# Output products of the last octet in every fourth segment: a buffer of their own in two pieces, and the left V products behind them

## The chip, the cores and the metric

One NeuronCore of a Trainium2 chip. The metric is the device time of one execution in microseconds; lower is better. Before the change three runs took 1659.49, 1665.99 and 1658.9 us (median 1659.49).

## The reference, cut to what matters

The output is a gated mix of a recurrent attention (A) and a gated feed-forward layer (B) over the same 2048 rows of width 640.

```python
def _A_ref(x, mem0, Wq, Wk, Wv, Wo, seg_len):       # 32 heads of 192, M = 8, seg_len = 32
    mem = mem0
    for s in range(n_seg):                           # 64 segments
        xs = x[:, s * seg_len:(s + 1) * seg_len, :]
        h = jnp.concatenate([mem, xs], axis=1)       # 40 rows
        q, k, v = (jnp.einsum('btd,dhe->bhte', h, W) for W in (Wq, Wk, Wv))
        scores = jnp.einsum('bhqe,bhke->bhqk', q, k) * scale
        scores = jnp.where(mask, scores, -1e9)
        p = _softmax(scores, axis=-1)
        o = jnp.einsum('bhqk,bhke->bhqe', p, v)
        o = jnp.einsum('bhte,hed->btd', o, Wo)
        mem = o[:, :M, :]                            # the next segment's memory
        outs.append(o[:, M:, :])
    return jnp.concatenate(outs, axis=1)

def _B_ref(x, w_gate, w_up, w_down):
    h = _gelu(x @ w_gate) * (x @ w_up)
    return h @ w_down

g = _sigmoid((x * gate_w).sum(-1, keepdims=True))
out = g * _A_ref(...) + (1 - g) * _B_ref(...)
```

The first eight rows that a segment puts out are the memory rows of the next one, so the 64 segments follow each other strictly.

## The kernel before

The feed-forward part runs first, with its result in a scratch tensor in memory. Then come the 64 segments. All instructions are added to one list in the order of the program; a small scheduler derives the semaphore waits from the regions that each operation reads and writes, and each engine runs its own instructions in the order in which they were added. Nothing is reordered later, so the lists `PROG`, `PROG1` and `PROG3` in the source are the order.

A segment handles its 32 heads as four *octets* of eight. For each octet there are three projections (Q, K and V, each in five steps over the width with four 128x384 products side by side in the array: items `("g", n, k)`, lines 1134 and 226), the transposes of the Q and K rows on VectorE (`tq`, `tk`, line 1172), the scores (`sc`, lines 1183 to 1198), the softmax (`ex`), the transpose of its weights (`pt`, lines 1245 and 1250, copied by ACT at line 1257 and DVE at line 1259 for the last octet), the head outputs (`pv`, function `pv_oct`, lines 1278 and 1280) and their products with Wo (`wo`). The V rows are copied out of PSUM by ACT at line 1158. Item `("wo", i, 0)` handles the first half of octet i, `("wo", i, 1)` the second. Odd segments go through the octets backwards in the weights, so that half of the weights can stay where they are; the rest of them, 13 pieces of Q, K and V and three of Wo, are loaded during the segment into the slots of pieces that the segment has used (line 631, on the queue of SP).

Each segment has 32 rows of its own in this scheme: the 24 first rows of x and the eight memory rows. The eight last rows of x of four segments (the *left* rows) are put together: their Q, K and V rows are worked out for four segments at once (`lf`, `le`, `vb`; the left V products of the next four segments are line 967), and their head outputs wait in `uTl` until the last of the four. Hence a segment has a *place*, s % 4, and the fourth place (q == 3, program `PROG3`) differs: there the output products take 64 columns of head outputs (40 of this segment and 24 collected left ones) in function `wo_both`, line 1372, into one bank, LB. Their stationary operand is the buffer `U3` of 1536 bytes per partition. Three writers fill it in `pv_oct`: POOL with the left columns (line 1292, "U3l"), ACT with two of three chunks of the head outputs (line 1310, "uT evac") and DVE with the third in the last octet (line 1315, "uT mid"). There is one `U3` for all four octets, so those writers wait until the products of the octet before have read it. At places one to three the last octet's copies are made by halves instead (lines 1300 and 1304), each of two output products' operand.

The end of a segment of the fourth place runs through: `("wo", 2, 0)`, `("wo", 2, 1)`, `("pv", 3)`, three fifths of the left V products, `("wo", 3, 0)`, `("wo", 3, 1)`, the other two fifths. Behind it the sums in bank LB are copied by DVE (line 1561) and ACT (line 1564), DVE transposes them into the next segment's memory rows (line 1572) and with that the next segment's first projection may start. DVE mixes the outputs (lines 1083, 1431) with what POOL has scaled (lines 1081, 1089). ACT copies the left V rows (line 958).

The working memory behind all this is one tensor, cut by the tables `wsA_off` and `wsB_off`. In it `Q` holds the transposed Q rows of the octet at work (960 bytes), `p` its softmax weights (512 bytes) and, next to it, `Qz` a zero-padded copy of part of Q.

## Time and profile before

| | |
|---|---|
| median of three runs | 1659.49 us |
| the profiled execution's own time | 1669.24 us |
| its span, from the first to the last instruction | 1667.5 us |
| mean granted TensorE clock in it | 0.996 |
| TensorE busy | 1566.5 us, 94% of the span |
| VectorE, ScalarE, GpSimd busy | 60%, 47%, 33% |
| moved by DMA | 499.28 MB |

In the rows of the profile, PE is TensorE's products, PEld its weight loader, DVE is VectorE, ACT ScalarE, POOL GpSimd, and SPq the queue of SP, which only issues loads and stores. A row in order of time has the start and the length in us, the engine, the line of the source, the operation with its operands, how many of them are merged in it, and in brackets how long the engine was idle ahead of it and what ended that. A row of a wait has who waited for whom, the total, how many times, and the longest. In a chain of waits, each step leads to what released the step after it.

### The profile page before, as it was taken

To read this page: it belongs to the slowest core of one execution; us is meant where nothing else is said; L and a number is where in the kernel's file an instruction comes from. 1 tells how busy PE (TensorE), PEld (TensorE's weight loads), DVE (VectorE), ACT (ScalarE), POOL (GpSimd) and SP (SyncE) were. 2 spreads that over 40 slices of the span, in tenths; PEclk is the share of its full clock that TensorE was granted. 3 is DMA by queue.
4 is the path that set the end of the run, shared out by engine and by line. 5 is a ranking of instruction groups with operands and counts; after the bars stand their busy time and mean duration, and the time that the engine had idled before them with its cause. 6 is when DMAs were issued, how large, how long until landed. Compare 5 with 4: busy or idle time off the path is not lost.

```text
span 1667.5 us, 75813 instructions
## 1 busy us (share of the span) xinstructions
PE 1566.5 (94%) x37107; PEld 779.2 (47%) x28147; DVE 1000.1 (60%) x3023; ACT 785.5 (47%) x1874; POOL 549.9 (33%) x1609
## 2 busy tenths in 40 slices
PE   9999899999999999999999999999999999999986
PEld 4444345444444445444455444454444454444533
DVE  6453566656566666666565666566665656656653
ACT  2222454545555454545455554455454555545442
POOL 1110233333333333333333333333333333333332
PEclk9999999999999999999999999999999999999999
DMA  9915899888889898988889898889888898888984
GB/s 297 340 43 160 323 321 330 301 282 310 324 317 325 300 319 290 334 306 311 303 305 343 315 327 289 303 315 340 308 302 310 308 336 311 307 297 308 324 312 179
DMA packets 275415, 499.28 MB, mean 299 GB/s; under 512 B 121119, under 2 KB 136327, under 8 KB 275079
## 3 DMA queue, kind: packets, MB, share of 16 engines
q1 hardware_dynamic: 271000, 491.30, 84.2%
q8 instruction: 255, 4.18, 1.0%
q10 hardware_dynamic: 4079, 3.14, 0.6%
q14 instruction: 81, 0.66, 0.1%
HBM read 473.25 MB, written 21.09 MB: 296 GB/s over the span
## 4 chain that ended last, share of the span: by engine, by line
PE 71%; DMA 17%; DVE 6%; ACT 3%; issue 3%; SPq 1%; POOL 0%; DVEq 0%; ACTq 0%; POOLq 0%
PE ps L1134 19%; PE ps L226 17%; DMA arena<-in_A_Wv_dram 9%; PE ps L1372 7%; DMA arena<-in_A_Wo_dram 6%; PE ps L1328 5%; PE ps L1278 3%; PE ps L835 3%; PE ps L832 3%; PE ps L1354 2%; PE ps L1183 2%; PE ps L926 2%; PE ps L858 2%; PE ps L1191 1%; DMA arena<-in_A_Wk_dram 1%
## 5 line engine op out<-in xcount | busy, mean ns | idle before, releaser
L1134 PE MATMUL ps<-arena 128*32 128x384 bf16 x8640 | 645.6, 328 | 28.0 <-DVE arena L1572 11.6
L226 PE MATMUL ps<-arena 128*32 128x384 bf16 x8960 | 639.7, 326 | 2.7 <-ACT arena L1155 1.2
L1134 PEld LDWEIGHTS ps<-arena 128*32 128x32 bf16 x8640 | 231.9, 96 | 399.2 <-issue 258.9
L1172 DVE STREAM_TRANSPOSE arena<-arena 128x384 bf16<-128x384 bf16 x512 | 273.6, 559 | 70.5 <-ACT arena L1155 69.3
L1155 ACT ACTIVATE arena<-ps 128x384 bf16<-128x384 f32 x512 | 230.4, 493 | 99.0 <-PE ps L1134 93.8
L1328 PE MATMUL ps<-arena 128*32 128x320 bf16 x3456 | 184.4, 300 | 16.2 <-issue 11.1
L1175 POOL COPY arena<-arena 64x160 bf16<-64x160 bf16 x256 | 81.9, 320 | 334.3 <-DVE arena L1172 332.8
L1210 DVE TENSOR_REDUCE arena<-ps 104x4 f32<-104x160 f32 x256 | 82.9, 324 | 162.3 <-PE ps L1198 162.0
L1158 ACT ACTIVATE arena<-ps 128x384 bf16<-128x384 f32 x256 | 124.9, 488 | 88.2 <-PE ps L1134 88.2
L1263 ACT ACTIVATE arena<-ps 128x448 bf16<-128x448 f32 x192 | 104.4, 544 | 125.3 <-PE ps L1250 125.3
L1222 ACT ACTIVATE ps<-ps 104x160 f32<-104x160 f32 x256 | 74.8, 292 | 177.0 <-DVE ps L1212 175.2
L1310 ACT ACTIVATE arena<-ps 128x480 bf16<-128x480 f32 (+1 forms) x208 | 116.7, 561 | 87.4 <-PE ps L1280 86.1
L1008 POOL COPY arena<-arena 128x96 bf16<-128x96 bf16 x256 | 70.2, 274 | 246.7 <-PE ps L1198 174.4
L1224 DVE TENSOR_REDUCE arena<-ps 104x4 f32<-104x160 f32 x256 | 82.9, 324 | 83.8 <-ACT ps L1222 82.4
L1372 PE MATMUL ps<-arena 128*64 128x320 bf16 x1536 | 122.6, 307 | 0.5 <-ACT arena L1310 0.5
L1278 PE MATMUL ps<-arena 128*64 128x160 bf16 x1536 | 116.9, 240 | 5.6 <-ACT arena L1155 3.4
L1328 PEld LDWEIGHTS ps<-arena 128*32 128x32 bf16 x3456 | 89.6, 96 | 62.2 <-issue 19.1
L926 PE MATMUL ps<-arena 128*32 128x384 bf16 x1280 | 109.6, 328 | 1.1 <-issue 0.8
L1280 PE MATMUL ps<-arena 128*64 128x64 bf16 x1536 | 103.7, 193 | 2.3 <-issue 1.9
L1400 ACT ACTIVATE arena<-ps 128x384 bf16<-128x384 f32 x120 | 57.3, 490 | 101.2 <-PE ps L926 48.9
L1318 POOL COPY arena<-arena 128x96 bf16<-128x96 bf16 x192 | 51.7, 270 | 159.8 <-ACT arena L1300 88.7
L1278 PEld LDWEIGHTS ps<-arena 128*64 128x64 bf16 x1536 | 81.2, 109 | 37.6 <-ACT arena L1158 14.4
(102 smaller groups left out, 2362.6 us busy)
## 6 DMA issues: line engine op xcount, KB each, us to landing
arena<-in_A_Wk_dram SPq DMA_DIRECT2D x335, 384.0 KB, 6.5
arena<-in_A_Wv_dram SPq DMA_DIRECT2D x335, 384.0 KB, 8.7
arena<-in_A_Wo_dram SPq DMA_DIRECT2D x205, 480.0 KB, 6.0
arena<-in_A_Wq_dram SPq DMA_DIRECT2D x209, 384.0 KB, 5.5
arena<-left_qk_scratch SPq DMA_DIRECT2D x126, 96.0 KB
left_qk_scratch<-arena SPq DMA_DIRECT2D x49, 192.0 KB, 5.4
left_qk_scratch<-arena SPq DMA_DIRECT2D x30, 96.0 KB, 5.5
ffn_b_scratch<-arena ACTq DMA_DIRECT2D x16, 160.0 KB, 4.1
```

Source lines behind the costliest of these rows:

```text
L226: return e.add_instruction(mybir.InstMatmult(name=nm, start_tensor_calc=like["start"], stop_tensor_calc=stop, tile_size=(128, 32), tile_po ...
L926: fns.append(lambda e, outp=outp, rhs=rhs, j=j: e.matmul(outp, lhs, rhs, start=(k == 0), stop=(k == KT - 1), tile_position=(0, 32 * j)))
L1134: fns.append(lambda e, outp=outp, rhs=rhs, j=j: e.matmul(outp, lhs, rhs, start=(k == 0), stop=(k == KT - 1), tile_position=(0, 32 * j)))
L1155: S_.add("act", lambda e, m=m, bk=bk: e.activation(out=rows_sb[m], in_=ps[:, bk, 0:384], func=ACTF.Copy), reads=[r_ps[bk]], writes=[r_rows ...
L1158: S_.add("act", lambda e, i=i, bk=bk: e.activation(out=v_sb[i % NVB].rearrange("p (c n) -> p c n", c=3), in_=ps[:, bk, 0:384].rearrange("p ...
L1172: S_.add("dve", lambda e: e.transpose(out=dst[:, :, 0:L], in_=rows_sb[m].rearrange("p (c r) -> p c r", r=L)), reads=[r_rows[m]], writes=[r ...
L1263: S_.add("act", lambda e: e.activation(out=PT, in_=ps[:, bank, 0:PTW + 128], func=ACTF.Copy), reads=[r_ps[bank]], writes=[r_PT], name="pT ...
L1278: return [lambda e: e.matmul(full, v[:, e0:e0 + 64], PTm[:, i], start=True, stop=False, tile_position=(0, 64 * i), skip_group_check=True), ...
L1280: lambda e: e.matmul(part, vl[:, e0:e0 + 64], PTl[:, i], start=False, stop=True, tile_position=(0, 64 * i), skip_group_check=True)]
L1310: S_.add("act", lambda e: e.activation(out=apx(u[:, 0, 0, :], [[rs, na], [3 * rs, 4], [1, R]]), in_=ps[:, A, 0:na * W].rearrange("p (c t r ...
L1328: fns.append(lambda e, i=i, t=t, j=j, gv=gv: e.matmul(ps[32 * j:32 * j + 32, bank, 0:2 * DJ].rearrange("p (h n) -> p h n", h=2), lhs2[i], ...
L1372: S_.add("pe", [lambda e, i=i, g_=g_, c=c, p=p: e.matmul(ps[64 * i:64 * i + 64, LB, 0:2 * DJ], U3[:, p % 4, c, :], g_[:, c, 2 * DJ * i:2 * ...
```

## The change

The fourth octet at the fourth place no longer uses `U3`. It gets a buffer of two pieces of 768 bytes, `U3h`, one for each pair of output products, in memory that is free by then: `Q` for one, `p` and the start of `Qz` for the other. POOL copies the left columns in two pieces, and ACT and DVE copy the head outputs by halves, as at the other three places. `wo_both` reads the fourth octet's operand from the pieces. Since the fourth octet's copies need not wait for the third octet's output products any more, `PROG3` moves `("pv", 3)` between the two halves of them, and all five fifths of the left V products behind the last output product. The assertion that the diff changes had asked at the fourth place that each octet's output products stand ahead of the next octet's head outputs; it now asks that for the first two octets only.

```diff
--- before.py
+++ after.py
@@ -427,6 +427,10 @@
     U3 = bview(wsB_off["uT"], 1536).rearrange("p (t c r) -> p t c r", c=3, r=64)
     r_U3 = sreg(wsB_off["uT"], 1536)
     r_U3p = [[sreg(wsB_off["uT"] + x + 4 * i, 4) for x in (0, UB)] for i in range(3)]
+    U3h = [bview(wsB_off[nm], 768).rearrange("p (t c r) -> p t c r", c=3, r=64) for nm in ("Q", "p")]
+    r_U3h = [sreg(wsB_off[nm], 768) for nm in ("Q", "p")]
+    r_U3hp = [[[sreg(wsB_off[nm] + x + 4 * i, 4) for x in xs_] for i in range(3)] for nm, xs_ in (("Q", (0, 8)), ("p", (0, 256, 512)))]
+    assert wsB["Q"] >= 768 and wsB_off["p"] + 768 <= wsB_off["K"]
     st_f = [[fview(wsA_off["stats"] + (2 * b + i) * 16, 16) for i in (0, 0, 1)] for b in range(2)]
     r_st = [sreg(wsA_off["stats"] + 32 * b, 32) for b in range(2)]
     uTl = bview(wsB_off["uTl"], NCH * XA * 2).rearrange("p (c t) -> p c t", t=XA)
@@ -541,8 +545,8 @@
             ("sc", 2), ("g", 4, 0), ("g", 4, 1), ("g", 4, 2), ("g", 4, 3), ("pt", 1), ("tq", 3), ("wo", 0, 0),
             ("ex", 2), ("g", 4, 4), ("wo", 0, 1), ("tk", 3), ("pv", 1), ("g", 5, 0), ("pt", 2), ("sc", 3),
             ("wo", 1, 0), ("ex", 3), ("wo", 1, 1), ("pv", 2), ("g", 5, 1), ("g", 5, 2), ("g", 5, 3), ("pt", 3),
-            ("g", 5, 4), ("wo", 2, 0), ("wo", 2, 1), ("pv", 3), ("vb", 0), ("vb", 1), ("vb", 2), ("wo", 3, 0),
-            ("wo", 3, 1), ("vb", 3), ("vb", 4)]
+            ("g", 5, 4), ("wo", 2, 0), ("pv", 3), ("wo", 2, 1), ("wo", 3, 0), ("wo", 3, 1), ("vb", 0), ("vb", 1),
+            ("vb", 2), ("vb", 3), ("vb", 4)]
     PROG1 = [item for item in PROG if item != ("ex", 3)]
     PROG1.insert(PROG1.index(("pv", 2)), ("ex", 3))
     PROGS = (PROG, PROG1, PROG, PROG3)
@@ -1287,24 +1291,30 @@
         S_.add("pe", fns, reads=[r_v[o % NVB], r_vl[oc], r_PT], writes=[r_ps[A]] + ([r_ps[B]] if B != A else []), name="PVa s%d o%d" % (s, o))
         na = 2 if o in USPLIT else 3
         q = s % 4
-        if q == 3:
+        if q == 3 and o < NOCT - 1:
             u, ru = U3, r_U3p
             S_.add("pool", lambda e: e.tensor_copy(
                 out=U3.rearrange("p t c r -> p (t c) r")[:, :, R:64], in_=uTl[:, 12 * oc:12 * oc + 12, :]),
                 reads=[r_uTl[oc]], writes=r_U3p[2], name="U3l s%d o%d" % (s, o))
+        if q == 3 and o == NOCT - 1:
+            for h in ((0, 1), (1, 0))[s % 2]:
+                S_.add("pool", lambda e, h=h: e.tensor_copy(
+                    out=U3h[h].rearrange("p t c r -> p (t c) r")[:, :, R:64], in_=uTl[:, 12 * oc + 6 * h:12 * oc + 6 * h + 6, :]),
+                    reads=[r_uTl[oc]], writes=r_U3hp[h][2], name="U3l s%d o%d" % (s, o))
         if o == NOCT - 2 and s + 1 < NSEG:
             ek_copy(s, (3,))
-        if o == NOCT - 1 and q < 3:
+        if o == NOCT - 1:
             assert na == 2 and o % NUB == 1 and WOP == 4
+            uh, rh, rs = ([u[:, 2 * h:2 * h + 2] for h in range(2)], [[[x] for x in y] for y in r_uThp], R) if q < 3 else (U3h, r_U3hp, 64)
             for h in ((0, 1), (1, 0))[s % 2]:
                 S_.add("act", lambda e, h=h: e.activation(
-                    out=apx(u[:, 2 * h, 0, :], [[R, 2], [3 * R, 2], [1, R]]),
+                    out=apx(uh[h][:, 0, 0, :], [[rs, 2], [3 * rs, 2], [1, R]]),
                     in_=ps[:, A, 0:2 * W].rearrange("p (c t r) -> p c t r", t=4, r=R)[:, :, 2 * h:2 * h + 2], func=ACTF.Copy),
-                    reads=[r_ps[A]], writes=[r_uThp[h][0]], name="uT evac s%d o%d" % (s, o))
+                    reads=[r_ps[A]], writes=rh[h][0], name="uT evac s%d o%d" % (s, o))
                 S_.add("dve", lambda e, h=h: e.tensor_copy(
-                    out=u[:, 2 * h:2 * h + 2, 2, 0:R],
+                    out=uh[h][:, :, 2, 0:R],
                     in_=ps[:, B, 2 * W:3 * W].rearrange("p (t r) -> p t r", r=R)[:, 2 * h:2 * h + 2]),
-                    reads=[r_ps[B]], writes=[r_uThp[h][1]], name="uT mid s%d o%d" % (s, o))
+                    reads=[r_ps[B]], writes=rh[h][1], name="uT mid s%d o%d" % (s, o))
         else:
             rs = R if q < 3 else 64
             S_.add("act", lambda e: e.activation(
@@ -1368,12 +1378,13 @@
     def wo_both(s, item):
         for p in wo_pairs(s, item):
             g_, rg_ = piece(s, (3, p))
+            u, ru = (U3h[p % 4 // 2][:, p % 2], r_U3h[p % 4 // 2]) if item[1] == NOCT - 1 else (U3[:, p % 4], r_U3)
             for c in range(3):
-                S_.add("pe", [lambda e, i=i, g_=g_, c=c, p=p: e.matmul(
-                    ps[64 * i:64 * i + 64, LB, 0:2 * DJ], U3[:, p % 4, c, :], g_[:, c, 2 * DJ * i:2 * DJ * (i + 1)],
+                S_.add("pe", [lambda e, i=i, g_=g_, c=c, p=p, u=u: e.matmul(
+                    ps[64 * i:64 * i + 64, LB, 0:2 * DJ], u[:, c, :], g_[:, c, 2 * DJ * i:2 * DJ * (i + 1)],
                     start=(p == NWP - 1 and c == 0), stop=(p == 0 and c == 2), tile_position=(0, 64 * i),
                     skip_group_check=True) for i in range(2)],
-                    reads=[rg_, r_U3], writes=[r_ps[LB]], name="Wb s%d p%d" % (s, p))
+                    reads=[rg_, ru], writes=[r_ps[LB]], name="Wb s%d p%d" % (s, p))
 
     late_at = ("g", 1, KT - 1)
     r_lsth = [sreg(lst_off[3] + 768 * m, 768) for m in range(2)]
@@ -1383,7 +1394,7 @@
         g_end = {mi: at(("g", n, KT - 1)) for n, ms in enumerate(GROUPS) for mi in ms}
         assert g_end[(2, 1)] < at(("wo", 0, 0))
         assert at(("sc", 2)) < at(("pv", 1))
-        assert all(at(("wo", i, 1)) < at(("pv", i + (1 if x == 3 else 2))) for i in range(NOCT - (1 if x == 3 else 2)))
+        assert all(at(("wo", i, 1)) < at(("pv", i + (1 if x == 3 else 2))) for i in range(NOCT - 2))
         n_wos.append(at([item for item in prog if item[0] not in ("lf", "le", "vb")][-1]))
         for u in range(2):
             if ("le", x, u, 1) not in prog:
```

## The prediction

> **What bounds the kernel now.** I read the page's shares first, then the chain of work that ended last, then the stretches of the segments of the fourth place, and then each engine's order of time over the end of one such segment (985.60 to 1008.76), which I follow to the end of this text.
>
> ```profile
> PE 1566.5 (94%) x37107; PEld 779.2 (47%) x28147; DVE 1000.1 (60%) x3023; ACT 785.5 (47%) x1874; POOL 549.9 (33%) x1609
> DMA  9915899888889898988889898889888898888984
> ...
> PE 71%; DMA 17%; DVE 6%; ACT 3%; issue 3%; SPq 1%; POOL 0%; DVEq 0%; ACTq 0%; POOLq 0%
> ```
>
> TensorE carries 71% of the chain, and the loads 17%, at eight or nine tenths in nearly every slice. So a saving on TensorE counts only where no load ends the same stretch. The columns of the next rows are the stretch and its length, then the busy time and instructions of each engine, the granted clock and the share of the DMA.
>
> ```profile
> 340.53:367.24 26.71, 24.07 (x510) 12.60 (x390) 13.28 (x43) 11.89 (x29) 9.98 (x27) 0.94 0.79 270
> ...
> 985.60:1008.76 23.16, 22.31 (x509) 12.07 (x389) 13.22 (x43) 11.92 (x29) 9.51 (x26) 1.00 0.85 309
> ...
> sum 352.58, PE 337.08 PEld 182.30 DVE 197.76 ACT 178.44 POOL 143.48; mean PE 22.47 PEld 12.15 DVE 13.18 ACT 11.90 POOL 9.57
> ```
>
> Fifteen segments of the fourth place have a successor. Their sum is 352.58, or 23.5 each; most stand at 23.16, one at 26.71. A length that repeats so exactly is set by the program's own chain and not by loads, whose landing varies. The chain over the end of 985.60:1008.76 (start, length, what):
>
> ```profile
> 1003.02 1.75 PE ps L1372 x24
> ...
> 1005.07 0.87 PE ps L967 x12
> 1005.94 1.77 PE ps L1372 x24
> ...
> 1007.74 0.31 DVE arena L1561
> 1008.08 0.31 DVE arena L1561
> ...
> 1008.46 0.26 DVE arena L1572
> ```
>
> There is no DMA in it. It runs from the output products of the third octet through the head outputs, 12 left V products (L967) and the output products of the fourth octet (the second L1372) to the copies and the transpose that make the next segment's memory rows. What stands ahead of that second L1372 row is paid; what stands behind it, up to the transpose, is cover.
>
> **The change, part by part.** TensorE's starts and lengths, and the weight loader's, with the idle time ahead and its releaser:
>
> ```profile
> 1002.95 1.82 PE L1372 MATMUL ps<-arena 128*64 128x320 bf16 x24
> 1004.61 0.24 PE L1278 MATMUL ps<-arena 128*64 128x160 bf16 x2
> ...
> 1005.00 0.94 PE L967 MATMUL ps<-arena 128*32 128x384 bf16 x12
> 1005.87 1.82 PE L1372 MATMUL ps<-arena 128*64 128x320 bf16 x24
> 1007.62 0.51 PE L967 MATMUL ps<-arena 128*32 128x384 bf16 x8
> 1008.76 0.35 PE L1134 MATMUL ps<-arena 128*32 128x384 bf16 x4 [0.62 <-DVE arena L1572]
> ```
> ```profile
> 1005.60 0.10 PEld L967 LDWEIGHTS ps<-arena 128*32 128x32 bf16 x2 [0.33 <-ACT arena L1310]
> 1005.87 1.50 PEld L1372 LDWEIGHTS ps<-arena 128*64 128x64 bf16 x24 [0.17 <-issue]
> ```
>
> From the first output product of the third octet to that of the fourth pass 1005.87 - 1002.95 = 2.92 us: 1.66 for 24 products, 0.39 for the head outputs, 0.87 for the 12 left V products, which hold a stall of 0.33 for the ACT copy of the head outputs and 0.17 after it.
>
> *Left V products to the end.* The 0.87 goes out of this piece. The 12 products come back behind the last output product. There TensorE has 1008.76 - 1007.62 = 1.14 until the transpose lets the next segment begin, and 8 products in it. Eight of them took 0.51, and 12 products of the same shape 0.67 (next row), so each four add 0.16 and 20 take 0.99. They fit: cost 0, and 0.1 where they just do not.
>
> ```profile
> 1002.09 0.67 PE L1134 MATMUL ps<-arena 128*32 128x384 bf16 x12
> ```
>
> *Head outputs ahead of the second half of the third octet's output products.* The own buffer makes this legal; the 24 products are now 12, the head outputs, 12. One more change between kinds of product is needed; I bound it by 0 and 0.17 (the loader's idle time ahead of the second L1372, put down to issue) and take 0.02, since both kinds here load weights of the one shape 128x64. The head outputs move up by 12 products, 0.83, to 1003.8. Their inputs come from here:
>
> ```profile
> 1002.20 0.57 ACT L1310 ACTIVATE arena<-ps 128x480 bf16<-128x480 f32 x1 [1.04 <-PE ps L1280]
> 1002.88 0.44 ACT L1257 ACTIVATE arena<-ps 128x320 bf16<-128x320 f32 x1
> 1003.21 0.48 ACT L1158 ACTIVATE arena<-ps 128x384 bf16<-128x384 f32 x1
> ```
> ```profile
> PEld ps L1278 <- ACT arena L1158: 14.4, 30, 0.5
> ```
>
> The weights' copy ends at 1003.32, the V copy at 1003.69, 0.1 ahead of the new start. This edge was covered by the 12 products that now stand behind it, and the wait on it is real elsewhere (30 times, 14.4 us). The copy L1310 ended at 1002.77 and the output products that waited for it began at 1002.95, so a signal costs up to 0.18: bounds 0 and 0.19 a segment. I take 0.05, near the lower, since the copy ends first.
>
> *The copies in two pieces.* ACT and DVE copy two pieces of half the width:
>
> ```profile
> L1300 ACT ACTIVATE arena<-ps x96: 297/302/306, 197.7 to 1628.4; 128x160 bf16<-128x160 f32 x96
> ...
> L1304 DVE CAST arena<-ps x96: 228/236/244, 197.6 to 1628.3; 128x80 bf16<-128x80 f32 x96
> ```
>
> These are the same copies in the other three places (nanoseconds least, median, most). On ACT 2 x 0.30 stands for one copy of 0.44 (its place in time is between the end of the head outputs, 1005.0, and 1005.60, where the loader's wait for it ends); but the first piece is ready 0.30 after the head outputs, and the next 12 output products (0.83) cover it; the second has another 0.87, the 12 products that read the first piece, ahead of it. Were the 12 covering products gone, the stall of 0.33 would be back.
>
> *The left rows on POOL.* One copy that had to wait for the output products of the third octet becomes two that wait for POOL alone:
>
> ```profile
> 1003.16 0.29 POOL L807 COPY arena<-arena 128x120 bf16<-128x120 bf16 x1 [0.16 <-POOL arena L1448]
> 1004.84 0.43 POOL L1292 COPY arena<-arena 128x288 bf16<-128x288 bf16 x1 [1.39 <-PE ps L1372]
> ...
> 1006.93 0.69 POOL L1081 TENSOR_SCALAR arena<-arena 128x160 bf16<-128x160 bf16 x1 [0.17 <-POOL arena L1076]
> ```
>
> They run from 1003.45, at most 0.43 each, and are done by 1004.3. Three things wait for them: the last product of the third octet (the whole fourth octet is queued behind it), ACT's second piece, which writes beside one of them and could begin at 1004.6, and the products that read that piece; all come later, cost 0. The mixes behind them on POOL move up. The next segment's first POOL copy waits for TensorE, ACT and DVE besides, but for work that ends before the transpose it waits for anyway; behind it are the left rows and zeros for the first scores. SP's order is not changed.
>
> *Each boundary* then gains 0.87 less 0.02 for the extra change of product and 0.05 for V: 0.80. Fifteen give 12.0.
>
> *The last segment* has no left V products; its output products wait in the open.
>
> ```profile
> 1658.27 1.82 PE L1372 MATMUL ps<-arena 128*64 128x320 bf16 x24
> ...
> 1660.64 0.22 PE L1280 MATMUL ps<-arena 128*64 128x64 bf16 x1 [0.26 <-POOL arena L1292]
> ...
> 1661.38 1.82 PE L1372 MATMUL ps<-arena 128*64 128x320 bf16 x24 [0.53 <-ACT arena L1310]
> ```
>
> Both waits, 0.26 and 0.53, go behind the 12 products: 0.8 gained.
>
> *Late loads.* The fourth octet's last three output pieces are loaded in the same segment:
>
> ```profile
> 997.49 1.54 SPq L631 DMA_DIRECT2D arena<-in_A_Wo_dram  x3
> ...
> arena<-in_A_Wo_dram SPq DMA_DIRECT2D x3, 480.0 KB, 6.5
> ...
> arena<-in_A_Wo_dram SPq DMA_DIRECT2D x3, 480.0 KB, 7.3
> ```
>
> The last is issued by 999.03 and, at 6.5 or 7.3 us (the answers for this segment and for one 277 us later), lands at 1005.5 to 1006.3. It is needed by the last six output products, from 1007.2 before and 1006.4 after. It cannot land after 1007.2, or a wait would show before; so a boundary loses between 0 and 0.8. By the two answers it is 0 to 0.1 late: I take 0.07, 1.0 us for all.
>
> *Sum*: -12.0 - 0.8 + 1.0 = -11.8. The profiled execution took 1669.24 (span 1667.5 and 1.7 around it), so 1657.4 in its like; it is 9.8 over the median of the runs, 1659.49, and holds load stalls like 340.53:367.24 that the median need not have. From the median: 1647.7.
>
> **The rivals.** *The next place's loads take it back.* The first place's segments are not of one length:
>
> ```profile
> 367.24:389.56 22.32, 22.13 (x614) 11.21 (x474) 15.58 (x49) 10.64 (x27) 7.92 (x24) 1.00 0.88 314
> ...
> 1468.97:1492.78 23.81, 22.11 (x612) 11.33 (x473) 15.53 (x49) 10.75 (x28) 8.00 (x24) 1.00 0.84 294
> ```
>
> At equal TensorE work (22.1) they take 22.32 to 23.81, so loads do end some. If those loads went by the clock on the wall, 15 x 0.80 would be lost and 1658.7 remain; half of it, 1653. Against: a segment's loads are issued as its own products free their slots, so they begin earlier with it, and the DMA share of the fourth place (0.85) leaves room at its end. [...]
>
> ```profile
> DMA packets 290, 0.81 MB, mean 406 GB/s; under 512 B 32, under 2 KB 32, under 8 KB 288
> ```
>
> *The fourth octet's inputs end it.* If V costs its 0.19, the twenty left V products 0.1 and the last load 0.33 each time (between its 0 and 0.8), a boundary gains 0.87 - 0.62 = 0.25, and 1659.49 - 3.8 - 0.8 = 1654.9 results. For it: three margins of about 0.1; against: the exact 23.16.
>
> *Slower: a load stall that drops the clock.* In 340.53:367.24 the granted clock falls to 0.94, and the segment is 26.71 - 23.16 = 3.55 longer. If starting the products ahead of the last load turned its wait into such a drop, it would cost 3.55 in each segment struck: from four (14.2) it eats the gain, with six (21.3) the kernel is slower, with eight 1676. Against: the wait worked out above is tenths of a microsecond. [...]
>
> *It does not do what it says*: the output products of the fourth octet still start after the same wait. Then only the last segment's 0.8 is left, 1658.7.
>
> **How the numbers follow.** Forecast 0.60, own range 1645 to 1651. Loads take it back 0.16, inputs end it 0.10, clock drops 0.08, nothing done 0.06. Half a per cent, 8.3 us, is about what a measurement tells from no change here (three runs spanned 1658.9 to 1665.99): faster means under 1651.2. The forecast falls there but for 0.02; of the loads' rival a quarter too: 0.58 + 0.04 = 0.62. Slower is the clock's rival and a little of the unforeseen: 0.09. The rest, 0.29, is same. The range runs from 1644.5 (0.87 everywhere, no late load: -13.9) to 1657, which takes in the inputs' rival and half of the loads'; left out are 1658.7 and slower, about 0.2.
>
> **What would show it.** Right: fourth-place segments at about 22.35; the gap between the last L1372-like product of a segment and the next segment's first product still 1.14, with all 20 L967 products in it; from the third octet's first output product to the fourth's 2.1 in place of 2.92; POOL's two copies at 1003.5, not behind TensorE. Wrong: a wait of the head outputs for ACT L1158 over 0.2, of output products for in_A_Wo_dram over 0.3 each time, first-place segments longer by what the fourth lost, or more stretches at 0.94.

## The result and the profile after

The changed kernel took 1647.49 us (median of 6 runs, 1646.34 to 1655.51), the kernel before 1662.18 in the 6 runs that stand beside them (1655.51 to 1669.81). The ratio is 0.9917 with a 95% interval of 0.9889 to 0.9944: by the ratio 13.8 us saved, between 9.3 and 18.4 (the medians differ by 14.7), against a forecast of 11.8. The profiled execution took 1648.11, its span 1646.4, at a clock of 0.996 as before.

The page of the changed kernel: busy time of each engine, the load of the DMA in 40 slices, and the shares of the chain.

```profile
PE 1558.3 (95%) x37107; PEld 770.5 (47%) x28147; DVE 997.6 (61%) x3039; ACT 786.3 (48%) x1890; POOL 552.5 (34%) x1625
DMA  9925899888899898988889898999888998989885
...
PE 66%; DMA 15%; DVE 7%; SPq 4%; ACT 4%; issue 3%; POOL 0%; DVEq 0%; ACTq 0%; POOLq 0%
```

TensorE has the same 37107 products and 8.2 us less of busy time. The loads' part of the chain is about the same (DMA and SPq together 19%, 18% before). ACT, DVE and POOL have 16 instructions more each, one for each segment of the fourth place.

The stretches of fourth-place segments of the changed kernel (columns as in the prediction):

```profile
698.86:724.46 25.60, 23.70 (x510) 12.43 (x390) 13.27 (x44) 11.68 (x30) 9.76 (x28) 0.93 0.81 282
973.98:996.19 22.21, 21.80 (x510) 11.96 (x388) 13.18 (x44) 11.70 (x30) 9.70 (x27) 1.00 0.89 323
1065.88:1089.58 23.70, 22.25 (x510) 11.80 (x390) 13.31 (x44) 11.60 (x30) 10.07 (x28) 1.00 0.86 304
...
sum 341.02, PE 331.66 PEld 179.61 DVE 198.62 ACT 174.18 POOL 146.43; mean PE 22.11 PEld 11.97 DVE 13.24 ACT 11.61 POOL 9.76
```

An undisturbed segment now takes 22.17 to 22.21 in place of 23.16, so 0.95 to 0.99 less. The fifteen take 341.02 in place of 352.58: 11.56 less, where fifteen times 0.97 would be 14.6. So some of the gain per segment is lost in segments such as the last one quoted; the others were between 22.22 and 23.24. One segment at a lowered clock is there as before (25.60 here, 26.71 there).

The end of the segment 973.98:996.19, TensorE and then the weight loader in order of time:

```profile
991.33 1.00 PE L1383 MATMUL ps<-arena 128*64 128x320 bf16 x12
992.17 0.24 PE L1282 MATMUL ps<-arena 128*64 128x160 bf16 x2
...
992.47 2.62 PE L1383 MATMUL ps<-arena 128*64 128x320 bf16 x36
995.01 1.00 PE L971 MATMUL ps<-arena 128*32 128x384 bf16 x20
996.19 0.35 PE L1138 MATMUL ps<-arena 128*32 128x384 bf16 x4 [0.18 <-DVE arena L1583]
```
```profile
992.12 0.11 PEld L1282 LDWEIGHTS ps<-arena 128*64 128x64 bf16 x2
...
992.44 2.32 PEld L1383 LDWEIGHTS ps<-arena 128*64 128x64 bf16 x36
995.01 0.61 PEld L971 LDWEIGHTS ps<-arena 128*32 128x32 bf16 x20 [0.25 <-issue]
```

The lines have moved by 4 to 11: L1383 is L1372 of before, L971 is L967, L1282 and L1284 are L1278 and L1280, L1138 is L1134. The 36 output products stand in one row: 12 of the third octet, then all 24 of the fourth, with no wait between. At 0.066 each (2.62 less a last product's 0.30, over 35) the fourth octet's first stands at 992.47 + 12 x 0.066 = 993.26. From 991.33 that is 1.93 us, 2.92 before. Behind the last output product 20 left V products lie in a gap of 996.19 - 995.01 = 1.18, and at its end TensorE still waits 0.18 for the transpose.

The copies of ACT, of DVE and of POOL in the same stretch, engine by engine:

```profile
991.59 0.48 ACT L1162 ACTIVATE arena<-ps 128x384 bf16<-128x384 f32 x1
992.68 0.50 ACT L1310 ACTIVATE arena<-ps 128x160 bf16<-128x160 f32 x2 [0.60 <-PE ps L1284]
```
```profile
992.68 0.39 DVE L1314 CAST arena<-ps 128x80 bf16<-128x80 f32 x2 [1.07 <-PE ps L1284]
```
```profile
991.83 0.68 POOL L1301 COPY arena<-arena 128x144 bf16<-128x144 bf16 x2
```

The V copy ends at 992.07 and the loader begins with the head outputs at 992.12, with no idle time marked. Yet its loads for the 12 products ahead ended at 992.01, so it stood for 0.11; in the kernel with the old order, below, it stands there for 0.02 (998.70 to 998.72). TensorE lost nothing by it: the 12 products ahead take 0.84 from start to start, about half of the 1.66 that 24 took before.

The second of ACT's two copies begins at 992.88 and takes 0.30, so the first piece is done by about 992.98 and both by 993.18. The head outputs are the operand that the weight loader reads; at (2.32 - 0.11) / 35 = 0.063 a load it comes to the first piece at 992.44 + 12 x 0.063 = 993.20, and TensorE at 993.26. The first piece has 0.2 to spare, both together are just in time. POOL is done at 992.51.

### The profile page after: what moved, and what is told of

It reads as the page before. It is cut to its first block, busy times and chain, and to the rows that moved or that the text cites. A ratio compares the mean times of both kernels' runs of the same rounds, so it can differ in the third digit from the quotient of the medians.

```text
span 1646.4 us, 75860 instructions
## 1 busy us (share of the span) xinstructions
PE 1558.3 (95%) x37107; PEld 770.5 (47%) x28147; DVE 997.6 (61%) x3039; ACT 786.3 (48%) x1890; POOL 552.5 (34%) x1625
## 4 chain that ended last, share of the span: by engine, by line
PE 66%; DMA 15%; DVE 7%; SPq 4%; ACT 4%; issue 3%; POOL 0%; DVEq 0%; ACTq 0%; POOLq 0%
PE ps L1138 18%; PE ps L226 17%; DMA arena<-in_A_Wv_dram 6%; PE ps L1383 6%; PE ps L1338 5%; DMA arena<-in_A_Wo_dram 5%; DMA arena<-in_A_Wk_dram 3%; PE ps L1282 3%; PE ps L1364 3%; PE ps L1187 2%; PE ps L930 2%; SPq L635 2%; PE ps L836 2%; PE ps L839 2%; PE ps L862 1%
## 5 line engine op out<-in xcount | busy, mean ns | idle before, releaser
L1138 PE MATMUL ps<-arena 128*32 128x384 bf16 x8640 | 641.4, 328 | 17.3 <-DMA arena<-in_A_Wv_dram 5.8
L1138 PEld LDWEIGHTS ps<-arena 128*32 128x32 bf16 x8640 | 226.3, 96 | 391.4 <-issue 262.9
L1320 ACT ACTIVATE arena<-ps 128x480 bf16<-128x480 f32 x192 | 109.7, 571 | 60.0 <-PE ps L1284 57.1
L1383 PE MATMUL ps<-arena 128*64 128x320 bf16 x1536 | 123.2, 306 | 0.9 <-DMA arena<-in_A_Wo_dram 0.7
L1282 PE MATMUL ps<-arena 128*64 128x160 bf16 x1536 | 118.1, 240 | 5.5 <-ACT arena L1159 3.4
L1338 PEld LDWEIGHTS ps<-arena 128*32 128x32 bf16 x3456 | 88.8, 96 | 53.9 <-ACT arena L1261 17.0
L1284 PE MATMUL ps<-arena 128*64 128x64 bf16 x1536 | 103.9, 193 | 1.6 <-issue 1.6
L1282 PEld LDWEIGHTS ps<-arena 128*64 128x64 bf16 x1536 | 81.6, 109 | 39.4 <-ACT arena L1162 14.4
```

The lines of the kernel that those rows point to most:

```text
L1138: fns.append(lambda e, outp=outp, rhs=rhs, j=j: e.matmul(outp, lhs, rhs, start=(k == 0), stop=(k == KT - 1), tile_position=(0, 32 * j)))
L1282: return [lambda e: e.matmul(full, v[:, e0:e0 + 64], PTm[:, i], start=True, stop=False, tile_position=(0, 64 * i), skip_group_check=True), ...
L1284: lambda e: e.matmul(part, vl[:, e0:e0 + 64], PTl[:, i], start=False, stop=True, tile_position=(0, 64 * i), skip_group_check=True)]
L1320: S_.add("act", lambda e: e.activation(out=apx(u[:, 0, 0, :], [[rs, na], [3 * rs, 4], [1, R]]), in_=ps[:, A, 0:na * W].rearrange("p (c t r ...
L1338: fns.append(lambda e, i=i, t=t, j=j, gv=gv: e.matmul(ps[32 * j:32 * j + 32, bank, 0:2 * DJ].rearrange("p (h n) -> p h n", h=2), lhs2[i], ...
L1383: S_.add("pe", [lambda e, i=i, g_=g_, c=c, p=p, u=u: e.matmul(ps[64 * i:64 * i + 64, LB, 0:2 * DJ], u[:, c, :], g_[:, c, 2 * DJ * i:2 * DJ ...
```

## The experiments

Eleven more measurements were made in three groups, each group on another chip and beside its own runs of the kernel before. The first question is which part of the change does the work: the buffer, the moved head outputs, or the moved left V products. The short diffs are against the changed kernel. The place where a segment's time is most exact is its undisturbed length, so I read that beside the total; the total scatters, as the kernel before, profiled once more, shows.

### The kernel before again

> The kernel before once more, for a second profile of it. My theory: fourth-place segments again mostly at 23.16 us; the sums of the first three places differ from those of the first profile (375.9, 368.6 and 358.6 us) by up to 5 us each way, since loads set them, and that is why totals differ by several us between executions of one kernel. Rival: these sums are the same within 1 us, so that their differences between kernels are the kernels' own.

It took 1661.94 against 1669.24 in the first profile, with the same program. The sum of its fifteen fourth-place segments:

```profile
sum 349.79, PE 335.79 PEld 180.82 DVE 197.77 ACT 178.71 POOL 143.31; mean PE 22.39 PEld 12.05 DVE 13.18 ACT 11.91 POOL 9.55
```

349.79 and 352.58 are two executions of one kernel. Added up in the same way, the segments of the first three places took 1098.0 and 1103.1. A difference of 5 us there, or 3 in the fifteen, is no effect of an edit. The undisturbed fourth-place segment is 23.15 to 23.16 in both.

### The whole change, twice more

> The whole change once more, beside the next ones. My theory (the pieces are worth nothing, the order everything): fourth-place segments mostly 22.17 to 22.25 us, total as in the kernel whose products wait for both pieces, a ratio of 0.992 to 0.996. Rival (reading by pairs is worth 5 us): ratio 0.990 to 0.9925, clearly under the 0.9952 of that kernel.

> The whole change beside the two kernels before. Fourth-place sum of fifteen 338 to 341 us, as in both profiles so far; total 12 us under before give or take 3.

Measured: 1652.32 (ratio 0.9912, 0.9887 to 0.9936) and 1649.7 (0.9918, 0.9890 to 0.9946). The saving holds in these two groups as in the first measurement. Two things were not as expected: 0.9912 lies in the range that was named for the rival of the copies by pairs (a later section answers that), and 1649.7 is 15.4 under the 1665.13 of its group, 13.7 by the ratio, where 9 to 15 was expected. The fifteen of the first of the two:

```profile
sum 338.25, PE 329.86 PEld 178.52 DVE 198.43 ACT 174.60 POOL 145.82; mean PE 21.99 PEld 11.90 DVE 13.23 ACT 11.64 POOL 9.72
```

The second gave 338.55. From 349.79 that is 11.5 and 11.2 less, as 11.56 was between the first two profiles.

### The buffer alone, in the old order

```diff
-            ("g", 5, 4), ("wo", 2, 0), ("pv", 3), ("wo", 2, 1), ("wo", 3, 0), ("wo", 3, 1), ("vb", 0), ("vb", 1),
-            ("vb", 2), ("vb", 3), ("vb", 4)]
+            ("g", 5, 4), ("wo", 2, 0), ("wo", 2, 1), ("pv", 3), ("vb", 0), ("vb", 1), ("vb", 2), ("wo", 3, 0),
+            ("wo", 3, 1), ("vb", 3), ("vb", 4)]
```

> The buffer of two pieces alone; the order of the fourth place is that of before. My theory (the gain is the order: head outputs ahead of 12 products that cover their copies, and left V products as cover at the end): little is gained, since the 12 left V products ahead of the fourth octet's output products stay and take about 0.5 us and a change of product; only the stall of 0.33 for the longer copy goes. Fourth-place segments mostly 22.95 to 23.05 us (before 23.16, after 22.21); total 2 to 3 us under before. Rival (the buffer's waits were the cost: POOL's and the writers' wait for the third octet's products): most of the gain is here, segments at 22.2 to 22.4.

Measured: 1664.17 against 1664.67, ratio 1.0003 (0.9981 to 1.0025); 11 of 15 segments between 23.02 and 23.07. TensorE and the loader at the end of one:

```profile
997.20 1.82 PE L1383 MATMUL ps<-arena 128*64 128x320 bf16 x24
...
999.25 0.81 PE L971 MATMUL ps<-arena 128*32 128x384 bf16 x12
999.99 1.82 PE L1383 MATMUL ps<-arena 128*64 128x320 bf16 x24
```
```profile
999.72 0.10 PEld L971 LDWEIGHTS ps<-arena 128*32 128x32 bf16 x2 [0.19 <-ACT arena L1310]
999.99 1.50 PEld L1383 LDWEIGHTS ps<-arena 128*64 128x64 bf16 x24 [0.17 <-DVE arena L1314]
```

From first to first product it is 2.79 (2.92 before): the copies by halves shorten the wait for ACT from 0.33 to 0.19, which is the whole 0.14. The left V products are still there as the cover of that wait. In the total 2 to 3 us were expected and nothing shows; 15 x 0.14 = 2.1 us lies inside the interval.

### The head outputs moved, the left V products where they were

```diff
-            ("g", 5, 4), ("wo", 2, 0), ("pv", 3), ("wo", 2, 1), ("wo", 3, 0), ("wo", 3, 1), ("vb", 0), ("vb", 1),
-            ("vb", 2), ("vb", 3), ("vb", 4)]
+            ("g", 5, 4), ("wo", 2, 0), ("pv", 3), ("wo", 2, 1), ("vb", 0), ("vb", 1), ("vb", 2), ("wo", 3, 0),
+            ("wo", 3, 1), ("vb", 3), ("vb", 4)]
```

> Buffer of two pieces and the head outputs between the halves of the third octet's output products; the left V products stay three ahead of the fourth octet's output products and two behind. My theory: the 12 left V products now cover nothing, as 12 output products have covered the copies already, and stand in the path with 0.5 us and two changes of product: segments 22.9 to 23.05, no better than the buffer alone; total 2 to 4 us under before. Rival (moving the head outputs is what pays, by the 0.33 and 0.17 of waits): segments at 22.5 or less.

Measured: 1660.44, ratio 0.9987 (0.9969 to 1.0004), least segments 22.88 to 22.90, some 0.27 below before. The loader:

```profile
999.46 0.28 PEld L971 LDWEIGHTS ps<-arena 128*32 128x32 bf16 x12 [0.25 <-issue]
1000.06 1.50 PEld L1383 LDWEIGHTS ps<-arena 128*64 128x64 bf16 x24 [0.32 <-issue]
```

No copy is waited for now. But the 12 left V products still stand in the path, with 0.25 of idle loader ahead of them and 0.32 behind, both put down to issue: the changes between the kinds of product.

### The left V products moved, the head outputs where they were

```diff
-            ("g", 5, 4), ("wo", 2, 0), ("pv", 3), ("wo", 2, 1), ("wo", 3, 0), ("wo", 3, 1), ("vb", 0), ("vb", 1),
-            ("vb", 2), ("vb", 3), ("vb", 4)]
+            ("g", 5, 4), ("wo", 2, 0), ("wo", 2, 1), ("pv", 3), ("wo", 3, 0), ("wo", 3, 1), ("vb", 0), ("vb", 1),
+            ("vb", 2), ("vb", 3), ("vb", 4)]
```

> Buffer of two pieces and all left V products at the end; the head outputs stay behind both halves of the third octet's output products. My theory: the products of the fourth octet start as soon as the first piece is copied, about 0.9 us after the first head output: TensorE stands still some 0.4 there, and segments are 22.75 to 22.85; total 5 to 7 us under before, about 0.6 a segment behind the whole change. Rival (the left V products' move is the whole gain): segments at 22.2 to 22.3, no stall ahead of the fourth octet's products.

Measured: 1656.65, ratio 0.9956 (0.9936 to 0.9975), undisturbed segment 22.78, 0.38 below before. TensorE:

```profile
997.45 0.24 PE L1282 MATMUL ps<-arena 128*64 128x160 bf16 x2
...
998.34 1.82 PE L1383 MATMUL ps<-arena 128*64 128x320 bf16 x24 [0.43 <-DVE arena L1314]
1000.10 1.00 PE L971 MATMUL ps<-arena 128*32 128x384 bf16 x20
1001.27 0.35 PE L1138 MATMUL ps<-arena 128*32 128x384 bf16 x4 [0.18 <-DVE arena L1583]
```

Here the cover is gone and the copies are waited for in the open, 0.43. So the three edits give 0.14, 0.27 and 0.38 from the kernel before, and the whole change 0.95 to 0.99. The first is contained in the other two; if the two moves only added to it, they would give 0.14 + 0.13 + 0.24 = 0.51. Another 0.44 or more comes only when the products stand over the copies *and* the left V products are out of the way.

These are figures of the undisturbed segment. The totals of this group do not show the last step: the kernel of the next section has the whole order and segments 0.61 shorter than this one, some 9 us in fifteen, and yet a ratio of 0.9952 beside 0.9956 here. In the other groups the whole order stands at 0.9906 to 0.9918. Whether scatter, the chip or the loads hide the step in the first group is not shown.

### Products that wait for both pieces

```diff
-            u, ru = (U3h[p % 4 // 2][:, p % 2], r_U3h[p % 4 // 2]) if item[1] == NOCT - 1 else (U3[:, p % 4], r_U3)
+            u, ru = (U3h[p % 4 // 2][:, p % 2], r_U3h) if item[1] == NOCT - 1 else (U3[:, p % 4], [r_U3])
...
-                    reads=[rg_, ru], writes=[r_ps[LB]], name="Wb s%d p%d" % (s, p))
+                    reads=[rg_] + ru, writes=[r_ps[LB]], name="Wb s%d p%d" % (s, p))
```

> The whole change, but the fourth octet's output products wait for both pieces. My theory: the second piece is copied 0.2 us after the first and just ahead of the end of the 12 covering products, so the pieces are worth 0 to 0.05 us a segment: segments 22.17 to 22.3, total that of the whole change within a us. Rival (the copies by pairs carry a good part of it): a wait of 0.2 us or more ahead of the fourth octet's products, segments at 22.4 or more.

> The kernel whose fourth-octet products wait for both pieces once more, on the chip and beside the runs of the next one. My theory (pieces worth nothing, the difference of the two ratios, 0.9952 and 0.9912, is scatter): total within 2 us of the whole change. Rival (the pieces are worth 4 us through a wait not seen at the fourth place): again 3 us or more over it.

Measured: 1655.79 (ratio 0.9952, 0.9926 to 0.9977) in the first group, in which the whole change did not run, and 1649.47 (0.9906, 0.9882 to 0.9931) in the third, beside 1649.7 for the whole change. The least segment is 22.16 in both, and 22.16 or 22.17 in the three profiles of the whole change. The fifteen in the third group:

```profile
sum 336.50, PE 329.43 PEld 178.97 DVE 198.46 ACT 174.21 POOL 145.17; mean PE 21.96 PEld 11.93 DVE 13.23 ACT 11.61 POOL 9.68
```

So waiting for both pieces costs nothing that shows, which fits the copies being finished at 993.18, just ahead of the loader at 993.20. The 3.5 us by which the first median lay above the whole change's of another group didn't come back beside it, so they are not the price of waiting for both pieces; what they are (the groups ran on different chips) is not shown. Copying in pieces is a different thing and was not taken out alone.

### The left V products twice

```diff
-            ("vb", 2), ("vb", 3), ("vb", 4)]
+            ("vb", 2), ("vb", 3), ("vb", 4), ("vb", 0), ("vb", 1), ("vb", 2), ("vb", 3), ("vb", 4)]
...
-                    if i == 0:
+                    if i == 0 and "v" not in lb:
```

> The whole change with the 20 left V products at the end done twice (the second time over the first, same result). Each four take 0.16 us, so the second 20 take 0.82, of which the idle time ahead of the next segment (0.18) hides a part: segments of the fourth place 22.75 to 22.9, against 22.2. My theory (the total follows the end of the fourth place in full): 15 x 0.6 = 8 to 10 us more than the whole change. Rival (the next places' loads absorb a good part of what is won or lost at the boundary): under 5 us more, and the sums of the first three places get shorter by the difference.

This asks two things: whether 20 products are about what the gap holds, and whether time added at the end of a fourth-place segment reaches the total or is taken up by the loads of the next place. Measured: 1657.77, ratio 0.9957 (0.9936 to 0.9977), beside 1652.32 for the whole change in the same group: 5.45 more. Two sums, of the fourth place and of fifteen segments of the first:

```profile
sum 346.46, PE 339.96 PEld 189.18 DVE 205.29 ACT 172.85 POOL 146.52; mean PE 22.66 PEld 12.61 DVE 13.69 ACT 11.52 POOL 9.77
```
```profile
sum 344.89, PE 332.64 PEld 168.02 DVE 226.52 ACT 166.87 POOL 118.35; mean PE 22.18 PEld 11.20 DVE 15.10 ACT 11.12 POOL 7.89
```

The undisturbed segment grows by 0.50 to 22.67, less than the 22.75 to 22.9 expected, and the fifteen by 8.2. The gap hides more than the 0.18 that is marked: a row of 8 left V products takes 0.51 (1007.62 before), one of 20 takes 1.00, so by estimate 20 add 20/12 of the 0.49 between them, 0.82, and TensorE's part of the gap that is free is 1.18 - 0.82 = 0.36. What is marked starts at the end of the last product; 1.00 - 0.82 = 0.18 of a row is that end, which overlaps with the next products when they follow at once.

The first place was 7.2 shorter than in the whole change's profile (352.11 for the same fifteen), which would speak for the rival of the loads; but it is one profile of each, VectorE too has 8.2 us less to do in these stretches (226.52 against 234.76, as a mix of outputs and the end of the transposes, which followed the boundary, now fall ahead of it), and of the 8.2 of the fourth place the medians show 5.45, the ratios 0.0045 x 1665 = 7.5. The expectation had 8 to 10 for the one and under 5 for the other. How much of a gain at the fourth place the loads of the first place take back isn't settled by this. It is not all of it.

### Without the late loads

```diff
+            if seg % 4 == 3 and other[0] == 3:
+                continue
```

> The whole change without the three loads of Wo pieces at the fourth place (its last output products and the first ones of the next segment then use pieces that lie there from before, so the output differs from the reference's). My theory (the late load of the last piece costs what the fourth-place segments above 22.2 show in part): segments nearer 22.17, no wait of TensorE for in_A_Wo_dram in them; 0.2 to 0.4 us a segment less on the mean, total 2 to 6 us under the whole change. Rival (the segments over 22.2 come from earlier pieces, not from the last Wo load): the fourth place's mean stays within 0.1 of the whole change.

What the output products of the fourth place wait for, in the kernel before, in the changed kernel and in this one (us in all, times):

```profile
  issue: 6.1, 33
  ACT arena L1310: 3.9, 15
```
```profile
  issue: 3.4, 18
  DMA arena<-in_A_Wo_dram: 3.4, 9
  ACT arena L1320: 3.4, 16
```
```profile
  issue: 3.7, 19
  ACT arena L1322: 3.0, 14
```

The wait for the load is new with the change: 3.4 us in nine places, 3.5 in 14 and 4.7 in 11 in the other two profiles of the whole change, and none before. Without the three loads it is gone, 11 of 15 segments stand between 22.16 and 22.21, and the time is 1642.02 (ratio 0.9860, 0.9837 to 0.9882), 10.3 below the whole change of its group, where 2 to 6 was expected. Not all of that belongs to the late load: the segment that closes the program also got 4.0 shorter (32.1 in place of 36.1 from its first projection to the end), since there TensorE's wait for POOL, which the next section is about, is 3.8 in place of 7.4. Two stretches of the fourth place:

```profile
1157.71:1180.30 22.59, 22.15 (x509) 12.14 (x389) 13.22 (x44) 11.79 (x30) 9.81 (x28) 1.00 0.73 253
1248.21:1273.99 25.78, 23.68 (x509) 12.55 (x390) 13.38 (x44) 11.62 (x30) 10.29 (x28) 0.93 0.68 233
```

With the second, at a clock of 0.93, the mean is 337.70 / 15 = 22.51, within 0.1 of the 338.25 / 15 = 22.55 of the whole change, which by the letter is the rival's sign; but the whole change's profile has no segment at a lowered clock. Without it the other fourteen average (337.70 - 25.78) / 14 = 22.28: 0.27 a segment, 4.0 us in fifteen. Of this the waits for the load were 3.5; the rest may come from the other loads, which have a freer queue here (a DMA share of 0.73 in place of 0.88). And a stretch at a clock of 0.93 came although no output piece was loaded there, so this late load isn't what makes such stretches.

### Past the change: the last segment

The last segment of the changed kernel, POOL and TensorE:

```profile
1632.41 1.08 POOL L1057 TENSOR_SCALAR arena<-arena 128x320 bf16<-128x320 bf16 x1 [7.70 <-DMA arena<-ffn_b_scratch]
1633.56 0.42 POOL L1296 COPY arena<-arena 128x288 bf16<-128x288 bf16 x1
```
```profile
PE ps L1202 <- POOL arena L1296: 8.0, 1, 8.0
```

POOL waits 7.70 us for a load that it needs only for the last mix of outputs; the copy of the left columns is queued behind that, and TensorE stands for 8.0. The kernel before has the same (`L1198 <- POOL arena L1292`, 7.2 us). The edit puts POOL's scaling behind the last head outputs:

```diff
             if item == ("pv", NOCT - 1) and q == 3 and s + 1 < NSEG:
                 mix_left_b(g)
+            if item == ("pv", NOCT - 1) and s + 1 == NSEG:
+                end_gates()
...
                 else:
                     end_load()
-                    end_gates()
```

> The whole change, and in the last segment alone POOL's gate copies and the scaling of the last rows (which wait for loads and held up its left rows, and with them TensorE, for 6.7 to 7.7 us) are put behind the fourth octet's head outputs. My theory (that wait ends the last segment, and no other work needs the scaled rows before): the last segment, from its first projection to the end of the span, falls from 35 to 36 us to 28 to 30 us, the last Wo loads being the next to wait for; total 6 to 8 us under the whole change, places unchanged. Rival (the Wo loads behind it end the segment at the same time): under 2 us gained.

Measured: 1641.85 (four runs, 1640.81 to 1646.95), ratio 0.9866 (0.9840 to 0.9893), beside 1649.7 and 0.9918 for the whole change in the same group. Its POOL:

```profile
1637.08 0.68 POOL L1301 COPY arena<-arena 128x144 bf16<-128x144 bf16 x2 [0.68 <-PE ps L1138]
...
1639.78 1.08 POOL L1057 TENSOR_SCALAR arena<-arena 128x320 bf16<-128x320 bf16 x1 [0.79 <-DMA arena<-ffn_b_scratch]
```

The wait for the load is 0.79 and stands behind the left columns. The last segment takes 25.8 from its first projection to the end, less than the 28 to 30 expected, and 34.9, 36.1 and 36.1 in three profiles of the changed kernel. The 34.9 begins at a clock of 1.00 (1610 to 1614), with rows of four products 0.16 to 0.17 apart, as the 25.8 does; like with like it is 9.0 us, of which the medians show 7.85. This kernel is the fastest of those that compute the whole.

## Why the prediction was right

**What bounds it.** Right: TensorE's own order, with no load in it, set the undisturbed segment. The copies of the head outputs and the left V products in the path were what went, as the two half-moves show.

**The boundary** was forecast to gain 0.80 (0.87 less 0.02 and 0.05) and gained 0.95 to 0.99; in the segment shown above it is 0.95. Where the 0.15 comes from:

- The change between products was charged with 0.02 and was a gain of 0.09. The head outputs cost 0.39 before and 992.47 - 992.17 = 0.30 now that products of the same weight shape stand on both sides. It is 0.30 too with the head outputs moved alone (998.25 to 998.55), and 0.40 with the buffer alone (998.85 to 999.25). The output products' idle time put down to issue, 6.1 us in 33 places before and 3.4 in 18 now, is no part of this: its 15 times 0.18 are the 0.17 ahead of the second L1372 row, which the 0.87 already held.
- The wait for the V copy was taken as 0.05, and TensorE shows none. (The list of waits has 14.4 us in 30 places for it in both kernels; the 0.11 for which the loader stands is not marked in it.) The upper bound of 0.19 did not come out of the prediction's rows: 1003.69 + 0.18 is 0.07 behind 1003.8. The delay from the copy's end to the loader was 0.05 (992.07 to 992.12).
- Behind the last output product it is 1.18 in place of 1.14, a loss of 0.04. The 20 left V products are not what fills it: TensorE waits 0.18 for the transpose at the end. That 0.04 was in none of my terms.
- The other 0.03 lie in the steps of the 24 products, 0.84 + 0.79 in place of 1.66.

**The copies in two pieces and POOL's two copies** cost nothing, as forecast. The 12 products are enough cover for the first piece (992.98 against 993.20 at the loader); for both pieces they are only just enough (993.18).

**The last segment** was forecast to gain 0.8. From the third octet's first output product to the fourth's it was 1661.38 - 1658.27 = 3.11 and is now 1.94, by these rows, so 1.17:

```profile
1638.33 1.01 PE L1383 MATMUL ps<-arena 128*64 128x320 bf16 x12
1639.17 0.23 PE L1282 MATMUL ps<-arena 128*64 128x160 bf16 x2
...
1639.47 2.62 PE L1383 MATMUL ps<-arena 128*64 128x320 bf16 x36
```

The same products in the same order take the same time here (1.94) as in the middle of the kernel (1.93). Of the 1.17, 0.79 are the two waits that I had added up. Nearly all of the other 0.38 belongs to the same two waits. The product ahead of the first one, in the kernel before:

```profile
1660.19 0.19 PE L1280 MATMUL ps<-arena 128*64 128x64 bf16 x1
```

The next one begins 0.45 later, at 1660.64, and from that to the output products at 1661.38 it is 0.74. With nothing to wait for such a product is followed after 0.03 (now 1639.44 to 1639.47). So the two waits cost 0.42 + 0.71 = 1.13: the marked wait starts at the end of the product ahead, and that product's own 0.2, which otherwise overlaps with the next ones, is lost with it.

**The late load** is the term that was too small: 0.07 a segment, 1.0 in all, against 3.4 to 4.7 us of waits and 4.0 by the experiment. The reason named was right (the load is needed 0.8 earlier, and is not issued earlier), and it lies inside the bounds of 0 to 0.8. But two answers about when a load lands are too few for a mean, and by those two (1005.5 and 1006.3, needed at 1006.4) it was not late at all: the 0.07 did not follow from them. One segment in which it struck, by TensorE's rows:

```profile
1085.34 2.21 PE L1383 MATMUL ps<-arena 128*64 128x320 bf16 x30
1087.91 0.60 PE L1383 MATMUL ps<-arena 128*64 128x320 bf16 x6 [0.36 <-DMA arena<-in_A_Wo_dram]
```

The last six output products, as the prediction had it, wait alone. So the sum over the fifteen, -12.0 + 1.0 = -11.0, came out at -11.2 to -11.6 by two errors that cancel: 2.6 more gained at the boundaries, and 3.0 to 3.3 lost inside the fifteen where 1.0 was forecast, for which the waits for the load are enough.

**The total.** 1647.7 was forecast and 1647.49 measured, but this is closer than the working deserves. The start was the median of three runs, 1659.49; all later medians of the kernel before are 1662.18 to 1665.19. The saving was 13.8 us, and 13.7 to 14.7 by the other two ratios, where 11.8 was forecast. The fifteen and the last segment explain 12.7 of it. The rest is smaller than the scatter of the first three places (1098.0 and 1103.1 for one program) and I can't place it.

**The rivals.** Nothing done: out. Inputs end it: out; of its three margins only the load's came near what it assumed (3.4 to 4.7 us of waits over fifteen are 0.23 to 0.31 a segment, 0.33 assumed). The clock: out; one segment of the fourth place is at a lowered clock in the first profile of each kernel and none in the later ones of either, and one came without the load that was to cause it. (The 985.60:1008.76 of the prediction kept 1.00 with 0.85 us of it idle; but waits of tenths of a microsecond also stood ahead of products at half their pace, as the end of the last section shows.) Loads of the next place take it back: not the whole gain, since some 0.8% stands in three measurements of the changed kernel; the first place took 377.9 to 379.5 in three profiles of the changed kernel against 375.9 and 376.0 before, while the second and third places were on the whole shorter. Some 2 us may be lost there, and the totals of the first group of experiments, which do not follow the segments, leave this rival a part. The row of 406 GB/s under it is the stretch from 997.3 to 999.3, in which the three late loads were issued; how much more could have been moved then, no run shows.

## What to carry to other kernels

A stall under a copy and a block of work used as its cover are one item: taking either away alone gave 0.27 and 0.38 of an undisturbed segment here, both together 0.95 to 0.99. If work is in the critical path only to cover a wait, look for products of the same path to stand there, and move the filler to where the engine waits anyway. When a stretch gets shorter, list the loads that are due inside it: one that had landed in time becomes a wait (3.4 to 4.7 us in 9 to 14 places here, none before), and a mean over many segments is needed for its price. And count a wait from start to start, against the same step without it: the 0.79 that were marked in the last segment cost 1.13.

## What the runs showed of the hardware

The changes between products with 64 columns of weights and those with 32 have a price here: the weight loader idles 0.25 us ahead of left V products that follow output products (995.01, and 999.46 with the head outputs moved alone), and 0.17 (1005.87 in the kernel before) or 0.32 us (1000.06 with the head outputs moved alone) ahead of output products that follow left V products, all of it put down to issue. Ahead of left V products that follow head outputs (1005.00 before) no idle time is marked, but TensorE's head outputs take 0.39 there and 0.30 between output products. Between head outputs and output products, which both load 128x64, none is marked either (992.12 and 992.44). So I had put the price on the wrong edge. That it is the change of weight shape, and not something else in which these kinds differ, no run here separates.

TensorE's 8 us of idleness in the last segment was followed by a lowered clock, as stretches of 2 us of the changed kernel show (the column ahead of the DMA share):

```profile
1628.00:1630.00 2.00, 0.00 (x0) 0.00 (x0) 0.00 (x0) 0.00 (x0) 0.00 (x0) 1.00 0.79 308
1630.00:1632.00 2.00, 0.00 (x0) 0.00 (x0) 0.00 (x0) 0.00 (x0) 0.00 (x0) 0.51 0.13 47
...
1634.00:1636.00 2.00, 1.96 (x17) 1.57 (x19) 1.18 (x5) 0.28 (x1) 0.00 (x0) 0.50 0.00 0
1636.00:1638.00 2.00, 2.00 (x40) 1.56 (x40) 0.37 (x2) 0.42 (x1) 0.42 (x1) 0.78 0.00 0
```

The clock is at 0.50 when work resumes at 1634.04 and at 1.00 in the 2 us from 1638 on. So the wait of 8.0 cost more than 8.0: the 24 output products at 1634.04 took 3.20 in place of 1.82. With the scaling moved behind, the same stretches keep 1.00, and the segment is 9.0 us shorter than in this profile. TensorE's last product ahead of the wait ended at 1626.1, and the clock is down from 1630 on, 3.9 us later; that it is back some 2.8 us after the work began again is an estimate from the 0.78 of 1636 to 1638. A slower pace also stood behind much shorter waits. In the second profile of the changed kernel the rows of four products at the start of the last segment begin 0.32 apart (1614.98 to 1617.86) and 0.16 to 0.17 apart from 1618.49 on, and the waits in the 3 us ahead of them were 0.49, 0.22 and 0.69. That its clock was near 0.50 there is an estimate from those steps. What lowered it is not shown.
